# Gated linear attention followed by SoLU: the order of the score products, of the masks and of one chunk's finish

## The chip, the cores and the metric

The kernel runs on one core of one Trainium2 chip. The metric is the device time of one execution in microseconds (us); lower is better. Before the change three runs gave 382.52, 382.90 and 383.46 us, a median of 382.9 us.

## The reference

The first block is a gated recurrence over 768 tokens for 4 batches and 8 heads of 48 columns; the second multiplies its output up to 1024 columns, applies a softmax-weighted product, normalises each row and multiplies down to 384 columns.

```python
# attention: q, k, v, alpha of (4, 8, 768, 48)
for t in range(S):
    state = alpha[:, :, t, :, None] * state + np.einsum('bhd,bhe->bhde', k[:, :, t], v[:, :, t])
    y[:, :, t] = np.einsum('bhd,bhde->bhe', q[:, :, t], state)
# x = y as (3072, 384)
h = x @ w_in
e = np.exp(h - h_max)
solu = h * e / (sum(e) + 1e-9)
ln = (solu - mean(solu)) / np.sqrt(var(solu) + 1e-6) * g_ln
out = ln @ w_out
```

## The kernel before, in words

**Tiling.** The 768 tokens are cut into six periods of 128 (index g, 0 to 5). A period of all four batches is 512 tokens, and each batch of it is one chunk, numbered n = 4g + b. The recurrence is done in blocks: scans build the running products of alpha, keys and queries are multiplied by them, and within a period the attention is a masked 128 by 128 product of keys and queries (`scores`, then `masked`), to which the part that reads the carried state is added.

**The heads' 48 columns.** They are split into a first 32 and a last 16. A batch takes 32 partitions, so the first 32 columns of a head fill one block of 32 rows; the last 16 of an even and an odd head share another. `apart` makes, from that shared block of queries, one copy with the odd head's rows set to zero and one with the even head's rows set to zero: two ScalarE multiplications by a parity column (line 248), the one for the even heads first. A score of a head is thus the sum of two matmuls over 32 rows, one of first rows (key block h, query block h) and one of last rows (key block 8 + h//2, query block 8 + h). The four batches use four different groups of 32 rows of the TensorE array, and each batch of a half of the heads has a PSUM bank of its own, `a0` to `a3`. These banks exist once (`ps_a` has one buffer per tag), so a second half of the scores can't begin in a bank before the mask multiplication has read the first half out of it. One call of `scores` is 32 matmuls; in the trace each fp32 matmul is two records, so 64.

**The two blocks overlap.** The kernel sets the order by hand. In the main loop over g = 1 to 5, step s (0 to 7) does `up(g, s)`: three products with `w_in` into a PSUM bank of `ps_h` (two buffers), then on ScalarE the exponential (line 404), on VectorE the product h times e (line 405), and on ScalarE its square (line 406). `running(g, s)` adds e and the square to running sums, e on GpSimd and the square on VectorE (line 421). `down` multiplies a half of a chunk by `w_out`, and `finish(n)` reads its result out: on VectorE a copy of a column, two tiny operations and, in period 0, a 128 by 384 addition of the mean (lines 519, 521, 524, 528), on GpSimd a power (line 532), on ScalarE a scaled copy (line 534), and on SyncE's queue the store (line 535). In between, the attention of period g + 1 is done, in pieces that a plan names. A plan has four places in a step: `head` ahead of `up`, `behind` after it (and ahead of `running`), `middle` after `running`, and `tail` after `down`. Period g = 1 uses the plan `first`, later ones `usual`. In g = 1 there is no `down` at all, since period 0 was multiplied down earlier.

**The work ahead of the loop.** Period 0's chunks 0 to 3 are finished one by one while the attention of period 1 is done. Right after `finish(3)` stand `scan_on(2, 2)` and `scan_on(2, 0)`, the forward scans of period 2: each takes a maximum (`least`, line 218), a reciprocal (line 219) and a scan of 516 columns (line 204), and the first of them a small copy before that (`fend`, line 215). Ahead of `finish(3)` are `keys_T(2)` and `keys(2)`, two transposes on VectorE and two products on GpSimd (line 228).

**The attention pieces of g = 1.** `on1` is the third forward scan, `lasts` and `firsts` transpose the queries on VectorE (lines 182, 179) and multiply them on GpSimd (`queries`, line 256), and store rows with DMAs of SyncE's queue (`move_lasts`, `move_firsts`, lines 235, 240); `decay` is a GpSimd product on the state, `read0` and `read1` read the state with matmuls into the banks a0 to a3, and `values` multiplies by the values.

Of the kernel before, what the change touches and what calls it, by code (L numbers as in the profile page):

```python
# [16 lines left out]
P = 128  # L17
# [15 lines left out]
def fast_path(ctx, tc, q, k, v, alpha, moe_w_in, moe_w_out, moe_g_ln, out):  # L33
# [13 lines left out]
    B, H, S, D = q.shape  # L47
# [4 lines left out]
    NP = H // 2  # L52
# [68 lines left out]
    qv = const.tile([P, 2 * H, SW], FP, name="qv")  # L121
    qe = const.tile([P, NP, SW], FP, name="qe")
    kT = const.tile([P, NB, P], FP, name="kT")
# [87 lines left out]
    def scan_on(g, i):  # L211
        part = slice(NP * i, NP * i + NP)
        s = seed[i % 2]
        if i == 2:
            nc.vector.tensor_copy(out=fend[:, g], in_=h4[:, :, 1])

        least = small.tile([P, NP, 1], FP, name="least")
        nc.vector.tensor_scalar(out=least, in0=h4[:, part, 1:2], scalar1=LEAST, scalar2=None, op0=ALU.max)  # L218
        nc.vector.reciprocal(out=s[:, :, 0:1], in_=least)
        scan(aT[:, part], aT[:, part], s, False)  # L220
# [47 lines left out]
    def quarter(b):  # L268
        return slice(32 * b, 32 * b + 32)

    def banks(name, shape, n=B):
        return [ps_a.tile([P] + shape, FP, tag=f"a{b}", name=f"{name}{b}") for b in range(n)]

    def scores(g, half, a=None):
        a = a or banks("a", [NP, P])
        for i in range(NP):
            h = half * NP + i
            for kb, qb in ((h, h), (H + h // 2, H + h)):
                for b in range(B):
                    nc.tensor.matmul(  # L280
                        a[b][:, i], lhsT=kT[quarter(b), kb], rhs=qv[quarter(b), qb, 0:P], start=kb == h, stop=kb != h,
                        tile_position=(32 * b, 0), skip_group_check=True,
                    )
        masks[half] = a
# [97 lines left out]
    def up(g, f):  # L382
        up_mm(g, f)
        up_act(g, f)
# [110 lines left out]
    def down(n, half, part=range(HF)):  # L495
        g, b = divmod(n, B)
        d = st[n]
        if half == 0 and 0 in part:
            d["o"] = ps_o.tile([P, 512], FP, tag="o", name="o")
        for f in (half * HF + i for i in part):  # L500
            nc.tensor.matmul(  # L501
                d["o"][:, 0 : DM + 1], lhsT=u_of(g, f)[:, b * P : b * P + P], rhs=w_out[:, f], start=(f == 0),
                stop=(f == FC - 1), skip_group_check=True,
            )

    def finish(n):
        g, b = divmod(n, B)
        d = st[n]
        s, o = sums[:, n], d["o"][:, 0:DM]
        t0 = b * S + g * P  # L510
        if g == G - 1:
            o_sb = work.tile([P, DM], FP, name="o_sb")
            r = gr[g]["r"][:, b : b + 1]
            nc.vector.tensor_scalar(out=o_sb[:, 0:P], in0=o[:, 0:P], scalar1=r, scalar2=None, op0=ALU.mult)  # L514
            nc.scalar.activation(out=o_sb[:, P:DM], in_=o[:, P:DM], func=AF.Copy, scale=r)  # L515
            nc.scalar.dma_start(out=out[t0 : t0 + P, :], in_=o_sb)
            d.clear()
            return
        nc.vector.tensor_copy(out=s[:, 0:1], in_=d["o"][:, DM : DM + 1])
        t = small.tile([P, 1], FP, name="t")  # L520
        nc.vector.scalar_tensor_tensor(
            out=t, in0=s[:, 0:1], scalar=-1.0 / DFF, in1=s[:, 0:1], op0=ALU.mult, op1=ALU.mult
        )
        nc.vector.tensor_tensor(out=s[:, 3:4], in0=t, in1=gr[g]["s"][:, b : b + 1], op=ALU.add)  # L524
        if g == 0:

            o = work.tile([P, DM], FP, name="o_mean")
            nc.vector.scalar_tensor_tensor(
                out=o, in0=mean_sb, scalar=s[:, 0:1], in1=d["o"][:, 0:DM], op0=ALU.mult, op1=ALU.add
            )  # L530
        r = small.tile([P, 1], FP, name="r")
        nc.gpsimd.tensor_tensor(out=r, in0=s[:, 3:4], in1=mhalf, op=ALU.pow)  # L532
        o_sb = work.tile([P, DM], FP, name="o_sb")
        nc.scalar.activation(out=o_sb, in_=o, func=AF.Copy, scale=r)  # L534
        nc.sync.dma_start(out=out[t0 : t0 + P, :], in_=o_sb)
        d.clear()
# [99 lines left out]
    def centre(f):  # L636
        nc.gpsimd.tensor_tensor(out=w_out[:, f, 0:DM], in0=w_out[:, f, 0:DM], in1=mean_sb, op=ALU.add)
# [51 lines left out]
    for i in (2, 0, 1):  # L689
# [6 lines left out]
        if i == 2:  # L696
            apart()
    scores(0, 0)
    t = [x.tile([P, NP, P], FP, tag=n, name="a_" + n) for x, n in ((ps_h, "h"), (ps_o, "o")) for _ in range(2)]
    scores(0, 1, t)  # L700
    read_begin()
    masked(0)
# [81 lines left out]
    move_firsts()  # L784
    down(2, 0)
    scores(1, 0)
    finish(1)
    decay(1)
# [14 lines left out]
    for i in range(3):  # L803
# [2 lines left out]
    keys(2)  # L806
    load(k, kn, 3)
    down(3, 1, (2, 3))
    finish(3)
    scan_on(2, 2)  # L810
    scan_on(2, 0)

# [3 lines left out]
        head={4: "keys_back", 5: "masked0", 6: "masked1"},  # L816
        behind={0: "v keys", 1: "on2 on0 on1", 2: "lasts firsts", 3: "apart", 5: "decay", 6: "alpha", 7: "back"},
        middle={6: "begin read0", 7: "values"},
        tail={4: "scores0", 5: "scores1", 6: "read1", 7: "kv"},
    )  # L820
    first = dict(
        head={3: "keys_back", 5: "masked0", 6: "masked1"},
        behind={0: "v", 1: "on1", 2: "lasts firsts", 3: "apart", 5: "decay", 7: "alpha back"},
        middle={7: "read1 values over"},
        tail={4: "scores0", 5: "scores1", 6: "begin read0"},
    )

    def attend(a, what):

        more = a + 1 < G  # L830
        if what == "v":
            load_v(a)
        elif what == "keys":
            keys_T(a)
            keys(a)
            if more:
                load(k, kn, a + 1)
        elif what[:2] == "on":
            scan_on(a, int(what[2]))
        elif what == "lasts":  # L840
            lasts(qn, qe[:, :, 0:P])
            ends_of_decay()
            queries(2)
            move_lasts()
        elif what == "firsts":
            firsts(qn, qv[:, 0:H, 0:P])
            queries(0)
            queries(1)
            move_firsts()
            if more:  # L850
                load(q, qn, a + 1)
        elif what == "apart":
            apart()
        elif what == "decay":
            decay(a)
        elif what == "keys_back":
            if more:
                keys_back(a)
        elif what[:6] == "scores":
            scores(a, int(what[6]))  # L860
        elif what[:6] == "masked":
            masked(int(what[6]))
        elif what == "alpha" and more:
            alpha_T(a + 1)
            if a > 2:
                attend(a, "over")
        elif what == "over" and more:
            alpha_over(a + 1)
            if a + 2 < G:
                load(alpha, an, a + 2)  # L870
        elif what == "back" and more:
            for i in range(3):
                scan_back(a + 1, i)
        elif what == "begin":
            read_begin()
        elif what[:4] == "read":
            read_state(int(what[4]))
        elif what == "values":
            read_values(a)
        elif what == "kv" and more:  # L880
            next_state(a)
# [3 lines left out]
    for g in range(1, G + 1):  # L885
        rise, att = g < G, g + 1 < G
        plan = first if g == 1 else usual

        def at(where, s):
            for what in plan[where].get(s, "").split() if att else ():  # L890
                attend(g + 1, what)

        after = None
        if not rise:
            break
        for s in range(FC):
            at("head", s)
            if rise:
                up(g, s)
            if after is not None:  # L900
                finish(after)
                after = None
            if s == 0 and g < 3:
                next_state(g)
            if s == 0 and g > 1:
                token_sums(g - 1)
            at("behind", s)
            for f in centres.get(s, ()) if g == 1 else ():
                centre(f)
            if rise and s:  # L910
                running(g, s)
            at("middle", s)
            if todo:
                n, half = todo.pop(0)
                down(n, half)
                if half:
                    after = n
            at("tail", s)
        if after is not None:
            finish(after)  # L920
        todo = [(n, half) for n in range(g * B, g * B + B) for half in range(2)]
# [493 lines left out]
```

## Time and profile before

The profiled execution took 382.77 us by its own time and has a span of 381.0 us; 1.77 us lie around the span.

| | busy us | share | instructions |
|---|---|---|---|
| PE (matmul) | 363.3 | 95% | 4341 |
| PEld (weight load) | 215.7 | 57% | 4341 |
| DVE (VectorE) | 251.2 | 66% | 413 |
| ACT (ScalarE) | 144.3 | 38% | 255 |
| POOL (GpSimd) | 112.1 | 29% | 122 |

The granted TensorE clock was full in the whole span. Times such as "at 124.45" are microseconds from the start of the span. The timeline lists merged instructions: start, duration, engine, line, operation, result and inputs, count, and in brackets how long the engine sat idle before it and what ended that. A merged row's duration runs from its first start to its last end; consecutive instructions overlap a little, so the distance of two starts is what an instruction costs in a row of them.

### The profile page before, as it was taken

The page shows a single profiled execution, that of the slowest core. Times are in us where ns is not written, and L with a number is a line of the kernel's source. Part 1 is how long each engine was busy: PE and PEld are TensorE (multiplying, and loading weights), DVE is VectorE, ACT ScalarE, POOL GpSimd, SP SyncE. Part 2 cuts the span into 40 slices and gives each one's busy share as a digit, 9 for nine tenths or more (in the row PEclk, how much of TensorE's full clock was granted, in tenths as well). Part 3 has the DMA queues.
Part 4 walks back from the last instruction along what each step waited for, and adds up shares of the span by engine and source line. Part 5 has one row for each costly group of instructions (what it writes and reads, how often), then busy time and mean ns, then how long its engine had stood idle before and what let it go on. Part 6 is the DMA issues. An engine that isn't in the chain of part 4 may idle for free. (4 is left out here: it accounts for less than half of the span.)

```text
span 381.0 us, 10060 instructions
## 1 busy us (share of the span) xinstructions
PE 363.3 (95%) x4341; PEld 215.7 (57%) x4341; DVE 251.2 (66%) x413; ACT 144.3 (38%) x255; POOL 112.1 (29%) x122
## 2 busy tenths in 40 slices
PE   8789899988999999999999999999999999999994
PEld 8675335656654656555665555665556565555552
DVE  0999878996999779884665875666874414444500
ACT  2628566681155436143261153341241132322100
POOL 6000000000243990455210465111475211332200
PEclk9999999999999999999999999999999999999999
DMA  9982978248239611927041627004023000000011
GB/s 181 179 322 88 204 208 207 44 95 184 66 88 190 149 44 46 199 64 181 2 105 47 142 69 168 21 5 96 10 77 78 22 2 21 23 22 21 22 45 48
DMA packets 72438, 36.05 MB, mean 95 GB/s; under 512 B 48184, under 2 KB 69952, under 8 KB 72384
## 3 DMA queue, kind: packets, MB, share of 16 engines
q1 hardware_dynamic: 71360, 34.39, 38.3%
q10 hardware_dynamic: 1024, 0.92, 0.7%
q8 instruction: 36, 0.59, 0.7%
q14 instruction: 18, 0.15, 0.1%
HBM read 25.30 MB, written 4.72 MB: 79 GB/s over the span
## 5 line engine op out<-in xcount | busy, mean ns | idle before, releaser
L390 PE MATMUL h<-x,w_in 128*128 128x512 f32 x288 | 133.4, 601 | 3.9 <-DVE room L405 2.7
L501 PE MATMUL o<-w_out,room 128*128 128x385 f32 x384 | 133.6, 492 | 1.1 <-DVE least L218 1.1
L501 PEld LDWEIGHTS o<-w_out,room 128*128 128x128 f32 x384 | 71.1, 189 | 56.0 <-issue 14.9
L390 PEld LDWEIGHTS h<-x,w_in 128*128 128x128 f32 x288 | 52.4, 189 | 63.3 <-issue 47.5
L405 DVE TENSOR_TENSOR room<-h,e 128x512 f32<-128x512 f32 x40 | 27.7, 693 | 58.1 <-ACT e L404 58.1
L404 ACT ACTIVATE e<-h 128x512 f32<-128x512 f32 x40 | 23.9, 597 | 88.9 <-PE h L390 88.7
L421 POOL TENSOR_TENSOR p<-p,e 128x512 f32<-128x512 f32 x30 | 40.8, 1361 | 26.5 <-ACT e L404 26.0
L406 ACT ACTIVATE u<-room 128x512 f32<-128x512 f32 x40 | 25.2, 630 | 44.0 <-DVE room L405 44.0
L532 POOL TENSOR_TENSOR r<-sums,mhalf 128x1 f32<-128x1 f32 x20 | 12.5, 626 | 86.9 <-DVE sums L524 86.8
L291 DVE TENSOR_TENSOR sT<-a,mask 128x512 f32<-128x512 f32 x44 | 27.3, 682 | 14.2 <-PE a L280 14.2
L421 DVE TENSOR_TENSOR p<-p,u 128x512 f32<-128x512 f32 x30 | 24.3, 810 | 8.4 <-ACT u L406 8.4
L280 PE MATMUL a<-qv,kT 32*128 32x128 f32 x704 | 24.9, 278 | 3.9 <-DVE least L218 1.8
L280 PEld LDWEIGHTS a<-qv,kT 32*128 32x128 f32 x704 | 22.0, 186 | 10.9 <-POOL p L421 2.2
L204 DVE TENSOR_TENSOR_SCAN hT<-aT,unit 128x516 f32<-128x516 f32 x18 | 22.2, 1278 | 8.3 <-ACT aT L677 8.3
L204 DVE TENSOR_TENSOR_SCAN aT<-aT,seed 128x516 f32<-128x516 f32 x18 | 24.4, 1355 | 0.6
L329 PE MATMUL y<-sT,vn 128*32 128x128 f32 x768 | 22.9, 274 | 0.8 <-issue 0.5
L329 PEld LDWEIGHTS y<-sT,vn 128*32 128x32 f32 x768 | 20.8, 110 | 4.2 <-issue 3.4
L228 POOL TENSOR_TENSOR kT<-kT,hT 128x1024 f32<-128x1024 f32 (+1 forms) x8 | 13.3, 1683 | 28.7 <-DVE kT L179 28.7
L196 ACT ACTIVATE sq<-an,mone 128x1536 uint8<-128x1536 f32 x12 | 18.9, 1574 | 0.2
L534 ACT ACTIVATE o_sb<-o,r 128x384 f32<-128x384 f32 x16 | 9.3, 581 | 25.1 <-POOL r L532 25.1
L243 POOL COPY qe<-hT 128x4 f32<-128x4 f32 x5 | 1.0, 191 | 58.5 <-DVE hT L204 58.5
L359 ACT COPY x<-y 128x384 f32<-128x384 f32 x24 | 11.2, 479 | 14.6 <-PE y L329 14.4
(142 smaller groups left out, 367.7 us busy)
## 6 DMA issues: line engine op xcount, KB each, us to landing
vn<-in_v_dram SPq DMA_DIRECT2D x24, 192.0 KB, 4.6
an<-in_alpha_dram SPq DMA_DIRECT2D x20, 192.0 KB, 4.5
out_dram<-o_sb SPq DMA_DIRECT2D x20, 192.0 KB, 1.9
room<-in_moe_w_in_dram SPq DMA_DIRECT2D x6, 512.0 KB, 7.7
room<-in_moe_w_out_dram SPq DMA_DIRECT2D x8, 384.0 KB, 4.4
kn<-in_k_dram SPq DMA_DIRECT2D x16, 192.0 KB, 4.4
qn<-in_q_dram SPq DMA_DIRECT2D x16, 192.0 KB, 4.4
lot<-qe SPq DMA_DIRECT2D x40, 64.5 KB, 2.1
```

The source lines that it names most:

```text
L196: nc.scalar.activation(out=sq, in_=x, func=AF.Relu, scale=sign, bias=mone, accum_out=over[:, g, i : i + 1])
L204: nc.vector.tensor_tensor_scan(out=o, data0=a, data1=s, initial=1.0, op0=ALU.mult, op1=ALU.add)
L228: nc.gpsimd.tensor_tensor(out=kT[:, part], in0=kT[:, part], in1=hk[:, part], op=ALU.mult)
L280: nc.tensor.matmul(a[b][:, i], lhsT=kT[quarter(b), kb], rhs=qv[quarter(b), qb, 0:P], start=kb == h, stop=kb != h, tile_position=(32 * b, 0 ...
L291: nc.vector.tensor_tensor(out=sT[:, b, half * NP : half * NP + NP], in0=a[b], in1=mask[:, None, :].to_broadcast([P, NP, P]), op=ALU.mult,)
L329: nc.tensor.matmul(y_bank(b)[quarter(r), a], lhsT=lhsT, rhs=rhs, start=(b, r) not in begun, stop=stop, tile_position=(row, 32 * r), skip_g ...
L390: nc.tensor.matmul(h, lhsT=w_in[:, a, f * P : (f + 1) * P], rhs=d["x"][:, a].rearrange("p b t -> p (b t)"), start=(a == 0), stop=(a == KC ...
L404: nc.scalar.activation(out=e, in_=h, func=AF.Exp)
L405: nc.vector.tensor_tensor(out=u, in0=h, in1=e, op=ALU.mult)
L406: nc.scalar.activation(out=u2, in_=u, func=AF.Square)
L421: eng.tensor_tensor(out=p, in0=d[0][i] if f == 1 else p, in1=d[f][i], op=ALU.add)
L501: nc.tensor.matmul(d["o"][:, 0 : DM + 1], lhsT=u_of(g, f)[:, b * P : b * P + P], rhs=w_out[:, f], start=(f == 0), stop=(f == FC - 1), skip ...
```

## The change

There are three edits.

- `scores` runs over all first rows of a half and then over all last rows, and in each pass over heads 0, 2, 1, 3 of the half. Before, it did first rows and last rows of one head after the other. Only the first matmul into a bank now carries the start flag; before, each head's first one did. The number of matmuls is the same, and the four batches stay the innermost loop.
- In the plan `first` (g = 1), the score products go from `tail` of steps 4 and 5 to `behind` of the same steps, and the mask multiplications go from `head` of steps 5 and 6 to `behind` of steps 4 and 5, right after the scores. As `tail` of a step and `head` of the next enclose no matmul of this period, the order of PE's instructions stays as it was; on VectorE the four masks now stand ahead of the step's `running` instead of behind it.
- `finish(3)` goes from ahead of the two forward scans of period 2 to behind `up(1, 0)` in the loop.

```diff
     def scores(g, half, a=None):
         a = a or banks("a", [NP, P])
-        for i in range(NP):
-            h = half * NP + i
-            for kb, qb in ((h, h), (H + h // 2, H + h)):
+        for last in range(2):
+            for i in (0, 2, 1, 3):
+                h = half * NP + i
+                kb, qb = (H + h // 2, H + h) if last else (h, h)
                 for b in range(B):
                     nc.tensor.matmul(
-                        a[b][:, i], lhsT=kT[quarter(b), kb], rhs=qv[quarter(b), qb, 0:P], start=kb == h, stop=kb != h,
+                        a[b][:, i], lhsT=kT[quarter(b), kb], rhs=qv[quarter(b), qb, 0:P], start=not last and not i, stop=bool(last),
                         tile_position=(32 * b, 0), skip_group_check=True,
                     )
...
     down(3, 1, (2, 3))
-    finish(3)
     scan_on(2, 2)
     scan_on(2, 0)
...
     first = dict(
-        head={3: "keys_back", 5: "masked0", 6: "masked1"},
-        behind={0: "v", 1: "on1", 2: "lasts firsts", 3: "apart", 5: "decay", 7: "alpha back"},
+        head={3: "keys_back"},
+        behind={
+            0: "v", 1: "on1", 2: "lasts firsts", 3: "apart", 4: "scores0 masked0", 5: "scores1 masked1 decay",
+            7: "alpha back",
+        },
+        tail={6: "begin read0"},
         middle={7: "read1 values over"},
-        tail={4: "scores0", 5: "scores1", 6: "begin read0"},
     )
...
-        after = None
+        after = 3 if g == 1 else None
```

The order of the instructions of GpSimd and of SyncE's queue does not change. ScalarE's changes in one place: the scaled copy of `finish(3)` goes from ahead of the first exponential of g = 1 to behind its square.

## The prediction

> **What bounds the kernel now.** I read the busy slices of the page first, then the windows by stage, the waits of PE, and at last the timelines of 105 to 150 us. In the page's slices PE is full almost everywhere:
>
> ```profile
> PE   8789899988999999999999999999999999999994
> DVE  0999878996999779884665875666874414444500
> ```
>
> The windows (PE, PEld, DVE, ACT, POOL busy, each with its count) say where it isn't:
>
> ```profile
> 120.00:140.00 20.00, 19.14 (x220) 10.37 (x218) 15.54 (x19) 8.07 (x15) 17.86 (x17) 1.00 0.51 116
> 160.00:180.00 20.00, 20.00 (x122) 11.43 (x121) 13.86 (x23) 7.66 (x15) 10.89 (x12) 1.00 0.58 133
> ```
>
> From 160 to 360 us PE never idles: only a changed number or rate of matmuls shows there. What edits two and three touch lies in period g = 1, 107 to 150 us, where PE still waits. Its timeline there:
>
> ```profile
> 114.83 2.84 PE L390 MATMUL h<-x,w_in 128*128 128x512 f32 x6 [0.80 <-DVE room L405]
> ...
> 124.45 0.60 PE L280 MATMUL a<-qv,kT 32*128 32x128 f32 x8 [0.31 <-POOL qv L256]
> 125.37 2.01 PE L280 MATMUL a<-qv,kT 32*128 32x128 f32 x56 [0.32 <-ACT qv L248]
> ...
> 130.09 3.43 PE L280 MATMUL a<-qv,kT 32*128 32x128 f32 x64
> 133.44 2.84 PE L390 MATMUL h<-x,w_in 128*128 128x512 f32 x6
> ```
>
> The reader is to see four losses: 0.80 at 114.83, where `up(1, 2)` waits for the product that frees its bank; 0.31 and 0.32 around the first scores; and a hidden one at 130.09, where 64 records hold PE for 3.35 us to the next start, though an undisturbed call (174.98 to 176.97, next start) takes 1.99, or 31.1 ns a record. That is 1.36 lost inside a row counted as busy. The cause is on VectorE:
>
> ```profile
> 127.84 1.18 DVE L421 TENSOR_TENSOR p<-p,u 128x512 f32<-128x512 f32 x1 [0.70 <-ACT u L406]
> 128.94 2.47 DVE L291 TENSOR_TENSOR sT<-a,mask 128x512 f32<-128x512 f32 x4
> ```
>
> The first scores were issued by 127.31, but the masks start at 128.94: ahead of them stands the running sum, which waited 0.70 for a square and was itself slow (1.18, elsewhere 0.67). The mask of bank a3 ends at 131.4, and only then can the fourth batch of the second scores begin.
>
> **What the Trainium skill says.** SBUF — State Buffer, section Who interferes with whom: VectorE's second SBUF port is shared with GpSimd under an exclusive lock, so a VectorE operation with two SBUF inputs, or a fast-mode copy, blocks until a GpSimd operation that reads SBUF is through. The trace agrees. Two tiny operations of `finish(3)` (0.16 each when alone) end as the GpSimd key products of 107.16 end, at 109.34 and 110.48:
>
> ```profile
> 107.16 3.32 POOL L228 TENSOR_TENSOR kT<-kT,hT 128x1024 f32<-128x1024 f32 x2 [8.12 <-DVE kT L179]
> ...
> 108.00 1.35 DVE L521 SCALAR_TENSOR_TENSOR t<-sums 128x1 f32<-128x1 f32 x1
> 109.39 1.11 DVE L524 TENSOR_TENSOR sums<-t,s 128x1 f32<-128x1 f32 x1
> ```
>
> The masks and the products of line 405 have one input in PSUM, so they pass. PSUM — Partial Sum Buffer, section Engine vs sequencer instructions: the queues of ScalarE, VectorE and GpSimd are strictly first in, first out, so a wait holds all behind it; the two lines from 127.84 show it.
>
> **Edit three, `finish(3)` behind `up(1, 0)`.** Before, VectorE did its four operations from 107.81 and the scan chain after them: `fend` 110.94, `least` 111.02, reciprocal 111.21, scan 111.42, second scan 112.97, product of `up(1, 0)` 114.12.
>
> After, `fend` and `least` come straight behind the transposes and take the two blocked slots: `fend` ends with the first key product (109.4), `least` with the second (110.5); elsewhere in the trace `least` took 0.73 under a GpSimd sum, so both kinds do block. The scan starts at 110.74, 0.68 earlier, and the product at 113.44. PE starts `up(1, 2)` at 114.15 instead of 114.83.
>
> The price comes behind. The four operations now follow that product: starts 114.02, 114.21, 114.40, 114.48 (spacings 0.19, 0.19, 0.08, from its other calls), then 0.52 for the mean. The power on GpSimd goes from 110.57 to 114.65, into an idle stretch (111.1 to 116.0), and ends at 115.20; ScalarE's scaled copy starts at 115.24 and now stands ahead of the exponential of `up(1, 1)`, which follows 0.52 later, at 115.76, where it was 115.35. So the product of `up(1, 1)` starts at 116.37, 0.41 later than its 115.96. VectorE itself is free by 116.0 (0.58 product, 0.98 finish, 1.0 state sums). From there VectorE has no gap until the query transposes end at 122.9, GpSimd's query products follow, and ScalarE's parity multiplications too: all 0.41 later. Scores begin at 124.86 instead of 124.45, and PE's 0.68 becomes a longer wait there. On SyncE's queue the store waits for the copy (to 115.9, was issued 115.13); the four loads of v behind it end their issue near 122.1 instead of 121.4, still ahead of the row moves, which wait for a query product at 122.6. That is covered.
>
> **Edit one, the order in `scores`.** At 124.86 first rows need no parity copy: 32 records to 125.86. The even copy is done at 125.7, the odd one at 126.34 (124.61 + 0.41 + 1.32), so even lasts run to 126.36 and odd ones, after some 0.07 of wait, end at 126.93. `up(1, 5)` starts then, 0.38 earlier than 127.31. In the other eleven calls the copies are long done and PE's spacing decides; row groups still rotate, and each fp32 matmul was two records into one place already, so I take zero. Bounds: the 12 transposes at 117.51 (122 ns each, full array) against 124 ns for four records leave 0.5 us to gain over 768 records; nothing excludes a loss, priced below.
>
> **Edit two, masks ahead of the running sum.** The product of `up(1, 4)` is at 126.86, the masks at 127.46 (0.60 apart, as between products and sums here), so a3's mask ends at 129.93 instead of 131.4. PE is through `up(1, 5)` at 129.71 and has to wait only to 130.0; 60 more records end at 131.9. `up(1, 6)` starts there, 1.5 earlier than 133.44.
>
> What is behind the masks: the running sum starts at 129.86, blocks on a GpSimd product and ends near 131.1; the next product starts at 131.0 (131.34 before), so it isn't late. The second masks wait for the scores and end at 134.5; GpSimd's `decay` ends near 133.9; `read0` can start at 134.7, with 1.5 kept. Late next would be the token sums of period 1, at 149.63 before and 148.1 now, which need the last running sum: 148.59 before, near 147.7 now, since its scans wait for the GpSimd sum that ends at 143.7. Slack 0.4, so the gain passes into the full stretch.
>
> **Sum.** 0.38 at 127 and 1.5 by 132 (not added: the second contains the first). Span 381.0 to 379.5, own time 382.77 to 381.3; the median of the runs is 0.13 above that execution, so **381.4 us**.
>
> **Rivals.**
> - *The finish costs more, or a later wait takes part of it back* (0.22). If the exponential of `up(1, 1)` is 1.0 late instead of 0.41, or the last running sum comes 0.6 to 1.0 after the token sums want it, 0.5 to 1.0 us remain: 382.2. For it: three VectorE operations and a GpSimd queue that meet in the lock at 130 and 137 us. Against: the slack of 0.4 at each.
> - *All of PE's waits go* (0.10). The four losses sum to 2.8, and a little is left on the PE side of 145 us (0.61 before `up(2, 0)`): 380.2. Against: the scores still wait for VectorE's chain.
> - *The new order slows the scores themselves* (0.11). Two passes might space the records wider. All 12 calls pay, most where PE is full: 2.0 ns more than 31.1 on 768 records eats the gain of 1.5, and from 3.5 ns the kernel is over 0.3% slower; at 4 ns, 384.5. For it: nothing shown; against: the rotation of row groups stays.
> - *Nothing moves* (0.05): the masks wait for something else than the running sum. The lines from 127.84 speak against it: 382.9.
>
> The likeliest case, 381.4, has the rest, 0.52, and its own range is 380.7 to 382.1, from the chain's delay of 0 to 0.9. A run can tell about 0.3% (1.15 us) from no change, so the border is at 381.75, near my value. About two thirds of the likeliest case and most of the full gain lie below it, with some of the first rival's better end and the scatter: faster 0.54, same 0.35, slower 0.11. The range over the cases is 380.3 to 383.0.
>
> **What would show it.** In the profile after: `up(1, 2)` near 114.1; first scores near 124.9 in one unbroken row of some 2.1 us, with no ScalarE wait inside; masks right behind the product near 127.5; the second scores lasting about 2.3 instead of 3.43; `up(1, 6)` near 131.9; token sums without a wait. Score calls after 160 us at 1.99 to the next start would clear edit one of harm. A scan at 111.4 as before, a mask that starts after 128.5, or a wait of PE for a running sum near 148 would make me wrong.

## The result, and the profile after

The changed kernel has a median of 381.13 us (8 runs) against 382.65 us for the kernel before beside it: 1.52 us less, ratio 0.9958, 95% interval 0.994 to 0.9975. The prediction was 381.4 us. A median also depends on how many of its executions had a lower granted clock of TensorE: of the eleven runs of the kernel before beside the last experiments, the six with a mean clock of 0.995 or 0.996 have a median of 383.9 us, the four with 0.999 or more 382.6. The profiled execution took 380.90 us and has a span of 379.0 us.

The page after, first and second part (busy, then the slices of PE), gives the change away as little as the page before gave the loss: PE has the same share, and 2.4 us less of busy time, since a stalled row of matmuls counts as busy.

```profile
span 379.0 us, 10060 instructions
...
PE 360.9 (95%) x4341; PEld 214.1 (56%) x4341; DVE 252.3 (67%) x413; ACT 144.2 (38%) x255; POOL 113.1 (30%) x122
...
PE   8688899988999999999999999999999999999994
```

The windows by stage of the kernel after: the later stretch is as full as it was.

```profile
160.00:180.00 20.00, 20.00 (x123) 11.59 (x121) 12.85 (x22) 8.21 (x15) 12.16 (x13) 1.00 0.47 115
```

The timeline of PE after, in g = 1 (lines of the file are one or more higher than before; 281 are the scores, 391 `up`, 457 the token sums):

```profile
110.28 5.69 PE L391 MATMUL h<-x,w_in 128*128 128x512 f32 x12
...
123.81 2.26 PE L281 MATMUL a<-qv,kT 32*128 32x128 f32 x64 [1.38 <-POOL qv L256]
126.01 2.84 PE L391 MATMUL h<-x,w_in 128*128 128x512 f32 x6
128.78 2.21 PE L281 MATMUL a<-qv,kT 32*128 32x128 f32 x64
130.92 2.84 PE L391 MATMUL h<-x,w_in 128*128 128x512 f32 x6
...
145.88 1.57 PE L368 MATMUL kv<-vn,kg 128*32 128x48 f32 x128
147.68 0.65 PE L457 MATMUL rows<-p,ones 128*32 128x64 f32 x32 [0.23 <-PE kv L368]
```

The last two rows in the kernel before:

```profile
148.25 1.57 PE L367 MATMUL kv<-vn,kg 128*32 128x48 f32 x128
149.63 0.64 PE L456 MATMUL rows<-p,ones 128*32 128x64 f32 x32
```

The reader is to see four things. `up(1, 1)` and `up(1, 2)` are one row of 12: the wait of 0.80 is gone. It comes back as 1.38 ahead of the first scores, where 0.31 stood. These are one row of 64, with no ScalarE wait inside. And the second scores take 2.14 to the next start instead of 3.35. At the end there is a new gap ahead of the token sums: from the state products (`kv`) to them it is 1.80 instead of 1.38.

The starts differ from trace to trace before anything that edits two and three touch: `up(1, 0)` starts at 107.03 before, at 106.12 after, and between 105.97 and 108.33 in the experiments. In three of them part of that is a spell of 3.4 us, between 20.0 and 24.3 us, with the granted clock at a half. So I compare distances between events, not their times since the span's start. Three distances cover g = 1 from the scans to the full stretch:

- A: from VectorE's 128x512 key transpose (line 182, ahead of the scans) to the start of the first scores. `finish(3)` acts here.
- B: from there to the start of `up(1, 6)`. Scores and masks act here.
- C: from there to the first `down` of the loop, behind the token sums. PE has next to no wait after that.

| kernel | A | B | C | sum | ratio of times (interval) |
|---|---|---|---|---|---|
| before | 17.59 | 8.99 | 16.76 | 43.34 | 1 |
| change, first trace | 17.58 | 7.11 | 17.34 | 42.03 | 0.9958 (0.994 to 0.9975) |
| change, second trace | 17.56 | 7.11 | 16.99 | 41.66 | 0.996 (0.9942 to 0.9978) |
| order alone | 17.59 | 9.00 | 16.77 | 43.36 | 0.9991 (0.9978 to 1.0003) |
| masks alone | 17.61 | 7.63 | 16.84 | 42.08 | 0.995 (0.9934 to 0.9966) |
| finish alone | 17.63 | 9.05 | 18.14 | 44.82 | 0.999 (0.9974 to 1.0006) |
| without finish | 17.61 | 7.11 | 16.86 | 41.58 | 0.9954 (0.9936 to 0.9972) |
| without order | 17.52 | 7.64 | 16.86 | 42.02 | 0.9977 (0.996 to 0.9993) |
| finish late | 16.56 | 7.11 | 17.80 | 41.47 | 0.9962 (0.994 to 0.9983) |
| finish late, sum first | 16.50 | 7.10 | 16.77 | 40.37 | 0.9907 (0.9872 to 0.9942) |
| sum first | 17.54 | 7.12 | 16.75 | 41.41 | 0.995 (0.993 to 0.997) |

The row "finish alone" is from its second trace; in it TensorE's clock fell to a half inside B, so its B and C are not to be read. The two traces of the change differ by 0.37 in their sums, nearly all of it in C, so a smaller difference in C or in the sum can't be told from scatter; A and B repeat to 0.02 there. The second trace of "finish late, sum first" has a sum of 40.38.

### The profile page after: what moved, and what is told of

It is laid out like the page before. It is cut to its first block, busy times and chain, and to the rows that moved or that the text cites. A ratio compares the mean times of both kernels' runs of the same rounds, so it can differ in the third digit from the quotient of the medians.

```text
span 379.0 us, 10060 instructions
## 1 busy us (share of the span) xinstructions
PE 360.9 (95%) x4341; PEld 214.1 (56%) x4341; DVE 252.3 (67%) x413; ACT 144.2 (38%) x255; POOL 113.1 (30%) x122
## 5 line engine op out<-in xcount | busy, mean ns | idle before, releaser
L422 POOL TENSOR_TENSOR p<-p,e 128x512 f32<-128x512 f32 x30 | 42.7, 1422 | 25.9 <-ACT e L405 25.6
L407 ACT ACTIVATE u<-room 128x512 f32<-128x512 f32 x40 | 25.2, 630 | 46.7 <-DVE room L406 46.7
L204 DVE TENSOR_TENSOR_SCAN hT<-aT,unit 128x516 f32<-128x516 f32 x18 | 23.5, 1352 | 8.4 <-ACT aT L678 8.3
L281 PE MATMUL a<-qv,kT 32*128 32x128 f32 x704 | 23.5, 277 | 4.4 <-DVE least L218 1.8
```

Of the source, the lines that this page charges most:

```text
L204: nc.vector.tensor_tensor_scan(out=o, data0=a, data1=s, initial=1.0, op0=ALU.mult, op1=ALU.add)
L281: nc.tensor.matmul(a[b][:, i], lhsT=kT[quarter(b), kb], rhs=qv[quarter(b), qb, 0:P], start=not last and not i, stop=bool(last), tile_posit ...
L407: nc.scalar.activation(out=u2, in_=u, func=AF.Square)
L422: eng.tensor_tensor(out=p, in0=d[0][i] if f == 1 else p, in1=d[f][i], op=ALU.add)
```

## The experiments

**One edit alone.** Each of the three edits was applied to the kernel before, as its part of the diff of the change stands; these three ran on one chip with the kernel that has the finish late.

The order in `scores`:

```diff
-        for i in range(NP):
...
+        for last in range(2):
+            for i in (0, 2, 1, 3):
```

> Edit one alone. My theory: the first scores of g = 1 end some 0.8 us earlier, but the masks still start near 128.9, behind the running sum, and the second scores wait for them, so up(1, 6) starts where it did before (133.4): 0.0, within 0.2 us of the kernel before. Rival, that the pass order itself makes scores cheaper or dearer: all calls after 160 us leave 1.99 us to the next start, and the time moves by over 0.5 us.

Measured: 382.62 us against 383.19, ratio 0.9991 with an interval that holds 1. PE's timeline of this kernel:

```profile
123.87 2.27 PE L281 MATMUL a<-qv,kT 32*128 32x128 f32 x64 [0.26 <-POOL qv L256]
126.07 2.84 PE L391 MATMUL h<-x,w_in 128*128 128x512 f32 x6
129.19 3.75 PE L281 MATMUL a<-qv,kT 32*128 32x128 f32 x64 [0.28 <-DVE sT L292]
132.87 2.84 PE L391 MATMUL h<-x,w_in 128*128 128x512 f32 x6
```

The first scores are through in 2.20, 0.66 sooner than the 2.86 before, and the second ones stand longer: 3.68 to the next start, and 0.28 ahead. B is 9.00 to 8.99 before: by the trace the gain is given back at once, as expected. The times alone could not tell 0.2 us from 0.8.

The masks:

```diff
-        head={3: "keys_back", 5: "masked0", 6: "masked1"},
+        head={3: "keys_back"},
...
+            0: "v", 1: "on1", 2: "lasts firsts", 3: "apart", 4: "scores0 masked0", 5: "scores1 masked1 decay",
```

> Edit two alone. My theory: the scores end at 127.3 as before, the masks follow at 127.4 instead of 128.9, the second scores run without a stall and up(1, 6) starts near 132.1: 1.1 to 1.4 us faster, near the whole gain of the change. Rival, that finish(3) brings the gain: 0.0 here.

Measured: 381.25 us (6 runs), ratio 0.995. By the trace B falls by 1.36, the size that the expectation gave. PE, and then VectorE, of this kernel:

```profile
124.54 0.60 PE L280 MATMUL a<-qv,kT 32*128 32x128 f32 x8 [0.33 <-POOL qv L256]
125.45 2.01 PE L280 MATMUL a<-qv,kT 32*128 32x128 f32 x56 [0.32 <-ACT qv L248]
...
130.17 2.07 PE L280 MATMUL a<-qv,kT 32*128 32x128 f32 x64
132.17 2.84 PE L390 MATMUL h<-x,w_in 128*128 128x512 f32 x6
```

```profile
126.53 0.69 DVE L405 TENSOR_TENSOR room<-h,e 128x512 f32<-128x512 f32 x1 [0.45 <-ACT e L404]
127.48 2.49 DVE L291 TENSOR_TENSOR sT<-a,mask 128x512 f32<-128x512 f32 x4 [0.26 <-PE a L280]
129.89 1.13 DVE L421 TENSOR_TENSOR p<-p,u 128x512 f32<-128x512 f32 x1
```

The second scores now take 2.00, an undisturbed call. What is left for the order is inside the first scores, which still take 2.86, and the masks wait 0.26 for them. By the times this edit alone is as fast as the whole change; by the sum it is 1.3 faster than before, where the change is 1.3 and 1.7.

`finish(3)` behind `up(1, 0)`:

```diff
-    finish(3)
     scan_on(2, 2)
...
-        after = None
+        after = 3 if g == 1 else None
```

> Edit three alone. My theory: up(1, 2) starts about 1 us earlier, PE then waits longer for the first scores, whose start hangs on VectorE's chain; that chain is delayed by 0.0 (as in the trace after) to 0.41 us (as predicted): 0.0 to 0.4 us slower. Rival, that PE's saved wait passes through: 0.7 to 1.0 us faster.

Measured: 382.47 us against 383.19, ratio 0.999, with an interval from 1.0 us faster to 0.2 slower. That excludes 0.4 slower, but not the rival's 0.7 faster; the trace does. `up(1, 2)` does not wait, the first scores wait 1.39, and A is 17.61, as before: PE's saved wait did not pass through. The clock fell within B in this trace, so a second one was taken:

> Edit three alone once more, for a trace: in the first one TensorE's granted clock fell to a half from 124.6 to 128, in the stretch to be read. Theory: up(1, 2) without a wait, the first scores at the same distance (17.6 us) from VectorE's query-key transposes (the 128x512 one ahead of the scans) as in the kernel before, the second scores held up by the masks as before.

The clock fell in the same place again, so only A (17.63) and `up(1, 2)` (no wait) can be read. That the masks hold up the second scores is not shown in this kernel; that the finish brings nothing rests on A and on the kernel without it below.

**The change less one edit.** In each of these two the part of the diff just shown, of `finish(3)` or of `scores`, is taken back out of the change. They ran on one chip with a second set of the change and with the combination below.

> The changed kernel itself, to stand beside the others of this call: 1.5 us faster than before (ratio 0.995 to 0.997).

Measured: ratio 0.996. Its trace repeats A and B of the first one to 0.02.

> Edits one and two, finish(3) where it was. Theory after the first traces: moving finish(3) leaves the start of the first scores where it was, because the 0.97 us of VectorE and 0.61 us of ScalarE that it puts into their chain equal what the scans gain; so this kernel is as fast as the change, within 0.3 us, with PE's wait of about 1 us ahead of up(1, 2) instead of 1.4 us ahead of the scores. Rival, that finish(3) has a share of the gain: 0.5 us or more slower than the change.

Measured: ratio 0.9954, as fast as the change. A, B and the waits came as expected:

```profile
114.00 2.84 PE L391 MATMUL h<-x,w_in 128*128 128x512 f32 x6 [1.03 <-DVE room L406]
...
123.64 2.26 PE L281 MATMUL a<-qv,kT 32*128 32x128 f32 x64 [0.33 <-POOL qv L256]
```

PE waits 1.03 ahead of `up(1, 2)` and 0.33 ahead of the scores here, 0 and 1.38 in the change: the same sum in another place. Edit three has no share in the gain that these traces show; the intervals of the two times would not tell 0.3 us.

> Edits two and three, scores in the old order. Theory: the first scores wait inside for the first parity copy and end some 0.8 us later than in the change, the masks start near 0.3 us later since they then wait for the scores instead of for the product; 0.2 to 0.5 us of the change's gain go. Rival, that the new order has no share once the masks are moved: equal to the change within 0.1 us.

Measured: ratio 0.9977, B longer by 0.53 than the change's. The size is as expected in the trace; in the times the difference to the change (0.0017, some 0.65 us) lies within the two intervals. With the masks moved the order is worth 0.5 in B; without, nothing. In the change part of that 0.5 is lost again in C, as the table shows; in the kernel without the finish (sum 41.58, masks alone 42.08) it is kept.

**Out of the chain.** `finish(3)` behind `up(1, 6)`:

```diff
-        after = 3 if g == 1 else None
+        after = None
...
+            if g == 1 and s == 6:
+                after = 3
             if after is not None:
                 finish(after)
```

> All three edits, but finish(3) stands behind up(1, 6) instead of up(1, 0), out of the chain of VectorE and ScalarE that leads to the first scores. My theory: the exponential of up(1, 1) no longer stands behind the scaled copy, the first scores start about 1.3 us earlier, right as PE gets there, and 0.8 to 1.3 us come on top of the change's 1.5: 2.3 to 2.8 us faster than before, less what the token sums wait for the last running sum. Rival, that another wait (GpSimd's query products or a transfer) sets the scores' start: same as the change, 1.5 us faster.

Measured: 381.76 us against 383.19, ratio 0.9962: by the times no faster than the change, and below what was expected. By the sum it is 1.9 less than before, 0.2 and 0.6 less than the change's two traces. The trace shows what was gained and what was lost. A fell by 1.0: the scores wait 0.31 again and `up(1, 2)` does not wait at all. But C grew by 1.04, nearly all of it ahead of the token sums, where PE waits 0.84. PE, VectorE and GpSimd of this kernel:

```profile
148.59 0.65 PE L457 MATMUL rows<-p,ones 128*32 128x64 f32 x32 [0.84 <-DVE p L422]
```

```profile
142.47 5.39 DVE L204 TENSOR_TENSOR_SCAN hT<-aT,unit 128x516 f32<-128x516 f32 x3
147.78 0.66 DVE L422 TENSOR_TENSOR p<-p,u 128x512 f32<-128x512 f32 x1
```

```profile
140.05 4.56 POOL L638 TENSOR_TENSOR w_out<-w_out,mean_sb 128x384 f32<-128x384 f32 x4
144.57 2.20 POOL L422 TENSOR_TENSOR p<-p,e 128x512 f32<-128x512 f32 x1
```

Three scans take 5.39 (3.40 before) while GpSimd centres weights and adds its running sum (2.20, alone 1.27). The last running sum is behind them in VectorE's queue, and the token sums wait for it. To tell whether that wait is all that took the gain back, the scans were put behind the sum:

```diff
-            7: "alpha back",
         },
         tail={6: "begin read0"},
-        middle={7: "read1 values over"},
+        middle={7: "alpha back read1 values over"},
```

> All three edits, finish(3) behind up(1, 6), and in step 7 of the first plan the transposes and back scans of period 3 behind the running sum instead of ahead of it. Theory: PE's wait for the last running sum ahead of the token sums (0.23 us in the change, 0.84 us with finish(3) late) is gone, and the two losses together bring 0.9 to 1.3 us on top of the change: 2.3 to 2.8 us faster than before (ratio 0.993 to 0.994). Rival, that the scans, now 1.3 us later, delay the next period's chain: no more than the late finish alone, 1.5 to 2.0 us faster.

Measured: 380.08 us against 382.81, ratio 0.9907, from 6 executions. As these are few, a second set was taken:

> The same kernel as late_sum once more, since few executions stood behind it: 2.3 to 2.9 us faster than before (ratio 0.992 to 0.994), and from the start of up(1, 0) to that of the first down of the loop about 40.2 us, where the kernel before took 43.2.

Measured: 379.66 us against 383.88, ratio 0.9905 (0.9883 to 0.9928); the distance that the expectation names is 40.34. PE of this second trace:

```profile
118.27 5.32 PE L391 MATMUL h<-x,w_in 128*128 128x512 f32 x12
123.86 2.27 PE L281 MATMUL a<-qv,kT 32*128 32x128 f32 x64 [0.27 <-POOL qv L256]
...
145.77 1.57 PE L368 MATMUL kv<-vn,kg 128*32 128x48 f32 x128
147.16 0.65 PE L457 MATMUL rows<-p,ones 128*32 128x64 f32 x32
```

No wait is left ahead of the token sums. By the sums of A, B and C this is 3.0 us less than before, of which the change has 1.3 to 1.7. The ratio says 3.6 us, with an interval of 2.8 to 4.5, but it is taken from a median of 383.9 of the kernel before; from the 382.6 of its runs at full clock (see the result) it is 3.0, as by the sums. It is faster than both kernels.

> The change, and in step 7 the transposes and back scans behind the running sum, finish(3) where the change puts it. Theory: the gap ahead of the token sums goes (0.42 us by distance of starts in one trace of the change, 0.11 in the other), so 0.1 to 0.4 us on top of the change, 1.6 to 2.0 us faster than before. Rival, that the order around the running sum by itself brings most of what late_sum brings: 2.5 us or more.

Measured: ratio 0.995 (0.993 to 0.997), 1.9 us. C is back to 16.75, A stays at 17.54. So putting the sum first is worth what the change loses ahead of the token sums, 0.2 and 0.6 by C (0.23 and 0.42 by the distance from the state products; the expectation's 0.11 is too low). The other 1.0 of the combination is `finish(3)`, which without the sum first brought 0.2 to 0.6.

## Why the prediction was right

**Where PE waited, and why: right.** The bound, the stall hidden in a busy row and its cause held. Masks alone bring 1.36 of B, the number read off that row.

**Edit two: right.** The masks start 0.61 behind the product (0.60 predicted), here on VectorE of the kernel after:

```profile
125.81 0.69 DVE L406 TENSOR_TENSOR room<-h,e 128x512 f32<-128x512 f32 x1 [0.45 <-ACT e L405]
126.42 2.47 DVE L292 TENSOR_TENSOR sT<-a,mask 128x512 f32<-128x512 f32 x4
128.81 1.50 DVE L422 TENSOR_TENSOR p<-p,u 128x512 f32<-128x512 f32 x1
130.22 0.68 DVE L406 TENSOR_TENSOR room<-h,e 128x512 f32<-128x512 f32 x1
```

From the first scores to `up(1, 6)` it said 7.04; it is 7.11.

**Edit one: right.** 2.07 predicted from the scores' start to `up(1, 5)`, 2.20 measured. Calls in the full stretch still take 1.99 to the next start (173.04 to 175.03 after), so the rival of slower scores falls.

**Edit three: right in its price, wrong in its gain.** The price from product to product of `up(1, 0)` and `up(1, 1)` was to be 2.93; it is 2.92 (1.84 before). What failed is the second half of the step "`fend` ends with the first key product (109.4), `least` with the second (110.5)". VectorE before and after, and the second key product after:

```profile
106.86 1.08 DVE L182 STREAM_TRANSPOSE kT<-kn 128x512 f32<-128x512 f32 x1
...
114.12 0.66 DVE L405 TENSOR_TENSOR room<-h,e 128x512 f32<-128x512 f32 x1
...
115.96 0.69 DVE L405 TENSOR_TENSOR room<-h,e 128x512 f32<-128x512 f32 x1 [0.26 <-ACT e L404]
```

```profile
106.23 1.09 DVE L182 STREAM_TRANSPOSE kT<-kn 128x512 f32<-128x512 f32 x1
107.18 1.55 DVE L215 COPY fend<-hT 128x12 f32<-128x12 f32 x1
108.65 0.16 DVE L218 TENSOR_SCALAR least<-hT 128x4 f32<-128x4 f32 x1
108.84 0.18 DVE L219 RECIPROCAL seed<-least 128x4 f32<-128x4 f32 x1
109.06 1.90 DVE L204 TENSOR_TENSOR_SCAN aT<-aT,seed 128x516 f32<-128x516 f32 x1
...
112.41 0.67 DVE L406 TENSOR_TENSOR room<-h,e 128x512 f32<-128x512 f32 x1
...
115.33 0.69 DVE L406 TENSOR_TENSOR room<-h,e 128x512 f32<-128x512 f32 x1 [0.34 <-ACT e L405]
```

```profile
108.67 1.20 POOL L228 TENSOR_TENSOR kT<-kT,hT 128x512 f32<-128x512 f32 x1
```

`least` started 0.02 ahead of the second product and took 0.16; the scan started behind it and was blocked instead, for 0.67 of its 1.90. Of the two operations of `finish(3)` whose slots `fend` and `least` were to take, the second waits for the first one's result and so starts behind the second product (0.10 behind it before). `least` needs nothing of `fend` and starts 0.08 before `fend` ends. From the transpose to the product it is 6.18 instead of 7.26, a gain of 1.08 where I had 0.68. Gain and price, 1.08 each, cancel, so the chain's delay is 0.0 (A), not 0.41.

**What followed behind: half right.** I left out one wait. GpSimd's `decay` waits 0.85 for the row moves' DMA:

```profile
132.29 1.65 POOL L264 TENSOR_TENSOR state<-state,lot 128x384 f32<-128x384 f32 x2 [0.85 <-DMA lot<-qv]
```

GpSimd gets there no earlier than before (25.2 us after the key transpose in both); the moves land later. In this trace the issue of the last four took 3.93 us on SyncE's queue instead of 2.47. Of the traces here, all with the masks moved but the second of "finish late, sum first" have some of this wait, 0.20 to 0.85, and none of the others has it. The kernel without order has it although that issue took 2.46, so why the moves land later stays open. It costs PE 0.16 in that trace, and nothing in the other (0.48 of wait). And the slack of 0.4 ahead of the token sums was mis-sized: I had the scans wait for GpSimd's last sum to end and then run free. VectorE and GpSimd there, before and after:

```profile
144.60 3.40 DVE L204 TENSOR_TENSOR_SCAN hT<-aT,unit 128x516 f32<-128x516 f32 x3
142.41 1.29 POOL L421 TENSOR_TENSOR p<-p,e 128x512 f32<-128x512 f32 x1
```

```profile
142.20 4.75 DVE L204 TENSOR_TENSOR_SCAN hT<-aT,unit 128x516 f32<-128x516 f32 x3
142.53 2.21 POOL L422 TENSOR_TENSOR p<-p,e 128x512 f32<-128x512 f32 x1
146.87 0.66 DVE L422 TENSOR_TENSOR p<-p,u 128x512 f32<-128x512 f32 x1
```

The sum began 0.33 us behind the first scan, and both were slow: 2.21 for the sum instead of 1.29, and 4.75 and 4.59 for the scans in the two traces instead of 3.40. The last running sum on VectorE then ends at 147.53, and the token sums start 0.15 later, the same 0.15 as in the kernel with the finish late, where the profile names that sum as what ended the wait. (In the kernel after it names PE's own products.) By the distance from the state products to the token sums, PE loses 0.42 and 0.23 beyond the 1.38 of the kernel before. That is the first rival's mechanism, below its price of 0.6 to 1.0, and one of the three signs that were to make the prediction wrong. The error in A made me expect 0.4 too little, the one in C 0.2 to 0.6 too much. That the sum still came out at 1.5 is in part luck: two errors of opposite sign.

By A, B and C the two traces give 1.3 and 1.7; the times give 1.52.

## What to carry to other kernels

A row of matmuls that counts as busy can hide a wait: compare the distance to the next start with that of an undisturbed row. Ahead of any operation that frees a single-buffered PSUM bank, nothing belongs in the queue that itself waits for another engine. An edit that moves work out of one wait brings nothing if the work lands in the chain that the next wait hangs on; follow the chain to where it may stand, and see what the earlier arrival runs into there.

## What the runs showed of the hardware

The lock on the port that VectorE and GpSimd share follows the order of the starts here, as the Trainium skill says (SBUF — State Buffer, Who interferes with whom: whoever issues first has the shared port for the whole instruction). In all nine traces with `finish(3)` moved, `least` started 4 to 17 ns ahead of GpSimd's second key product and ran at 0.16, and the scan started 0.39 to 0.41 behind that product and ended 1.09 behind its end. In the kernel before, the tiny operation at 109.39 started 0.10 behind the product, and it waited. Where both engines have a row of such operations they take turns: in the kernel after, the first scan ends at 143.67, GpSimd's sum 1.07 later, the second scan 1.09 after that.

TensorE's granted clock fell to a half for 3.4 us in some executions. In both profiles of the kernel with edit three alone it did so right after the first scores' wait of 1.4 us; here by windows (clock third from the end):

```profile
124.60:126.20 1.60, 1.55 (x28) 1.55 (x32) 1.14 (x2) 1.09 (x2) 1.60 (x2) 0.55 0.43 102
126.20:128.00 1.80, 1.80 (x37) 1.57 (x29) 1.10 (x2) 0.63 (x1) 1.72 (x3) 0.50 0.48 109
```

56 records of the scores took 3.33 us there, 2.01 in the kernel before. The change has the same wait (1.38 and 1.34) and its traces show no such spell, so whether the wait brings it on stays open.
